# One row shift for each pair of heads in place of two, and the first product of a main score tile issued twice while no gated unit runs

## The chip, the cores and the metric

The kernel runs on one core of a Trainium2 chip. The time is device time in microseconds for one execution. Five engines work side by side, each through its own queue in order: TensorE (PE in the profile; its weight loads are PEld), VectorE (DVE), ScalarE (ACT), GpSimd (POOL) and SyncE (SP), which here only issues DMA transfers. Three runs of the kernel before gave 1223.69 to 1225.79 us, with a median of 1224.95.

## The reference

An attention with the queries averaged in twos, over 8 batches and 8 heads, followed by a gated unit with a spatial product. Cut to what matters:

```python
# q, k, v: (8, 8, 1152, 64)
q_pool = q.reshape(B, H, S // 2, 2, D).mean(axis=3)          # 576 queries
scores = scale * q_pool @ k.T                                # 576 x 1152
scores = scores - max(scores, axis=-1)                       # row shift
attn = exp(scores); attn = attn / (sum(attn) + 1e-9)
x = (attn @ v), heads side by side                           # (8, 576, 512)

h = relu(x @ w_in)                                           # 1024 wide
u, v = h[..., :512], h[..., 512:]
v_n = (v - mean(v)) / sqrt(var(v) + 1e-6)
v_s = einsum('ts,bsd->btd', w_spatial, v_n) + b_spatial
out = (u * v_s) @ w_out
```

## The kernel before

**Pairs.** The 64 heads are worked in 32 pairs: two heads of one batch lie on the 128 partitions (64 each). For pair `i` the kernel prepares the operands (`prep`), finds each query's largest score (`maxima`), computes scores and exponentials (`attention`), and multiplies by the values (`values`, `tail_values`). Numbers are held as a high and a low half, so most products are made of several.

**Maxima and shift.** The 2 x 576 = 1152 queries of a pair are 9 blocks of 128: blocks 0 to 3 are the first 512 of head 0, block 4 the last 64 of head 0 and the first 64 of head 1, blocks 5 to 8 the rest of head 1. `maxima` computes for each block three products of 384 keys (L617, in block 4 L608) into a PSUM bank and takes the row maximum of each with VectorE (L623), into `mt`. `shift(st, mt, a, z)` then takes blocks `a` to `z`: the maximum over three pieces (L635, `mx`), a transposition on TensorE (L639), subtraction and scaling (L642), a cast and a remainder (L645, L646, `mr`), and two DMA transfers on SP (L649) that put the two halves as two extra rows into `X` (the buffers `xq`). The score products read these rows, so that the shift is part of the product. `maxima` calls `shift` for blocks 0 to 4 when block 4 is done and for blocks 5 to 8 at its end.

**Attention.** A pair has 18 main tiles (9 chunks of 128 keys for each head, 512 queries) and 4 tail tiles for the remaining 64 queries. A main tile is two products into one PSUM bank `pss` of three: L796 on the high halves, which opens the sum, and L797 on the low halves and the shift rows. L797 is thus the first that waits for the shift of its queries. ScalarE then takes the exponential (L802, into one of eight buffers `pt`), GpSimd splits the result into two halves (L822), and 12 products with the values follow (L714, L720, L725).

**Gated units.** When 8 pairs are done (two batches), a gated unit over these batches is put into the list `units` (`gated_unit`) and runs in small steps beside the attention of later pairs; the last one runs alone at the end. During the first 8 pairs, and into the ninth, the list is empty. In that time the weights of the gated units are also turned from doubles into two halves (`load_weights`, `from_double`, `head`, `rest`), mostly on VectorE and ScalarE.

**What sets the order.** The program is written as generators that take turns: `maxima(i + 1)`, `values_ahead(i)` and `prep(i + 2)` advance with each step of `attention(i)`. At the end `Order.pin` goes through the whole program with a cost for each instruction, takes on each engine the earliest ready one (the first in the program among these), and fixes the order that results on all five engines. So an instruction added or removed in one place can move others everywhere. On the chip each engine works through its own fixed row and waits at an instruction until its inputs and its buffer are there.

Of the kernel before, what the change touches and what calls it, by code (L numbers as in the profile page):

```python
# [261 lines left out]
def attn_sgu_kernel(ctx: ExitStack, tc: tile.TileContext, qT, kT, v, w_in, w_spT, b_sp, w_out, out):  # L262
    nc = tc.nc
# [13 lines left out]
    NT = S2 // P  # L277
# [316 lines left out]
    def maxima(i):  # L594
        st = state[i]
        qhl, khh, X = st["qhl"], st["khh"], st["X"]
        W = KEYS // 3
        NB = W // P
        mt = sm.tile([P, NT, 3], F32, name="mt", bufs=2)
        for t in range(NT):  # L600
            for n in range(3):

                if units or (t + n) % 2:
                    pm = ps_m.tile([P, 512], F32, name="pm")
                else:
                    pm = ps_w.tile([P, 512], F32, name="pw")
                if t == 4:
                    nc.tensor.matmul(  # L608
                        pm[:, :W],
                        lhsT=qd[i % 2].rearrange("p h s -> p (h s)"),  # L610
                        rhs=st["kn"][:, n * NB : (n + 1) * NB, :],
                        start=True, stop=True,
                    )
                else:
                    h = 0 if t < 4 else 1
                    c0 = t * P if t < 4 else TAIL + (t - 5) * P
                    nc.tensor.matmul(  # L617
                        pm[:, :W],
                        lhsT=qhl[:, h, c0 : c0 + P],
                        rhs=khh[:, h, n * NB : (n + 1) * NB, :],  # L620
                        start=True, stop=True,
                    )
                nc.vector.reduce_max(out=mt[:, t, n : n + 1], in_=pm[:, :W], axis=AX.X)  # L623
                yield

            if t == 4:
                yield from shift(st, mt, 0, 5)
        yield
        yield from shift(st, mt, 5, NT)

    def shift(st, mt, a, z):
        X = st["X"]
        n = z - a
        mx = sm.tile([P, NT], F32, name="mx", bufs=2)
        nc.vector.reduce_max(out=mx[:, :n], in_=mt[:, a:z], axis=AX.X)  # L635
        yield
        yield
        pt = ps_m.tile([P, 512], F32, name="pm")
        nc.tensor.transpose(out=pt[:n, :P], in_=mx[:, :n], identity=ident)  # L639
        mr = sm.tile([NT, 2, P], F16, name="mr", bufs=2)  # L640
        m = pt[:n, :P]
        nc.vector.tensor_scalar(  # L642
            out=m, in0=m, scalar1=st["lnp"][:n], scalar2=1.0 / MROW, op0=ALU.subtract, op1=ALU.mult
        )
        nc.vector.tensor_copy(out=mr[:n, 0], in_=m)  # L645
        nc.vector.tensor_sub(mr[:n, 1], m, mr[:n, 0])  # L646
        for r in range(2):
            rows = X[D + r : D + r + 1].rearrange("p h s -> p (h s)")
            nc.sync.dma_start(out=rows[:, a * P : z * P], in_=mr[:n, r])  # L649
        yield  # L650


    MAINS = (slice(0, MAIN), slice(TAIL, S))
# [13 lines left out]
    units = []  # L667
# [91 lines left out]
    def tail_values(i):  # L759

        b, hp = divmod(i, NHP)
        ptl, vp = state[i]["ptl"], vps[i % 2]
        ps = ps_m.tile([P, 512], F32, name="pm")
        o = ps[:, : 2 * D1].rearrange("p (h d) -> p h d", d=D1)
        for c in range(NC):
            top = ptl.bitcast(BF16)[:, c].rearrange("p h s -> p (h s)")[:, 1::2]
            rst = ptl.bitcast(F16)[:, c].rearrange("p h s -> p (h s)")[:, 0::2]
            nc.tensor.matmul(o, lhsT=top, rhs=vp[:, :, c, D : D + D1], start=c == 0, stop=False)
            nc.tensor.matmul(o[:, :, 0:D], lhsT=top, rhs=vp[:, :, c, 0:D], start=False, stop=False)
            nc.tensor.matmul(o, lhsT=rst, rhs=vp[:, :, c, D : D + D1], start=False, stop=c == NC - 1)  # L770
        r = inverse(o[:, 0, D : D + 1], "dent")
        for h in range(2):
            rows = slice(h * D, (h + 1) * D)
            nc.vector.tensor_scalar_mul(xt[rows, hp, rows], o[rows, h, 0:D], r[rows])

    def turn(last=False):

        while todo and (last or len(todo) > LAG):
            if not last and todo[0][1] % NC == 0 and len(todo) <= LAG + 1:
                break  # L780
            values(*todo.popleft())
        for x in list(later):
            x[0] -= 1
            if x[0] <= 0 or last:
                later.remove(x)
                x[1]()

    def attention(i):

        st = state[i]  # L790
        qhl, khh, X, KL, esc = (st[n] for n in ("qhl", "khh", "X", "KL", "esc"))
        ptl = pt_.tile([P, NC, 2, TAIL], F32, name="ptl")
        st.update(ptl=ptl, pt=[])

        def products(o, c, h, q):
            nc.tensor.matmul(o, lhsT=khh[:, h, c, :], rhs=qhl[:, h, q], start=True, stop=False)  # L796
            nc.tensor.matmul(o, lhsT=KL[0:KR, h, c, :], rhs=X[0:KR, h, q], start=False, stop=True)  # L797

        def main_tile(pt, c, h):
            ps = ps_s.tile([P, MAIN], F32, name="pss")  # L800
            products(ps, c, h, MAINS[h])
            nc.scalar.activation(pt, ps, AF.Exp, bias=0.0, scale=esc)  # L802

        def tail_tile(h, n):
            ps = ps_s.tile([P, MAIN], F32, name="pss")
            a, z = CUT[n], CUT[n + 1]
            cols = [ps[:, (c - a) * TAIL : (c - a + 1) * TAIL] for c in range(a, z)]
            for c, x in zip(range(a, z), cols):
                nc.tensor.matmul(
                    x, lhsT=khh[:, h, c, :], rhs=qhl[:, h, TAILS[h]], start=c == a, stop=False, skip_group_check=True  # L810
                )
            for c, x in zip(range(a, z), cols):
                nc.tensor.matmul(  # L813
                    x, lhsT=KL[0:KR, h, c, :], rhs=X[0:KR, h, TAILS[h]], start=False, stop=c == z - 1,
                    skip_group_check=True,
                )
            o = ps[:, : (z - a) * TAIL].rearrange("p (c s) -> p c s", s=TAIL)
            nc.scalar.activation(ptl[:, a:z, h], o, AF.Exp, bias=0.0, scale=esc)  # L818

        def split(t):  # L820

            nc.gpsimd.tensor_sub(t.bitcast(F16)[..., 0::2], t, t.bitcast(BF16)[..., 1::2])  # L822

        for k in range(STEPS):
            h, c = divmod(k, NC)
            st["pt"].append(pp.tile([P, MAIN], F32, name="pt"))
            main_tile(st["pt"][k], c, h)
            split(st["pt"][k])
            yield
            todo.append((i, k))  # L830
            turn()
            yield
            if k in (1, 2, 3, 4):
                tail_tile((k - 1) % 2, (k - 1) // 2)
                yield
            if k == TAIL_SPLIT:
                split(ptl.rearrange("p c h s -> p c (h s)"))
            if k == TAIL_AT:
                tail_values(i)
# [258 lines left out]
    next(norms[3])  # L1098
    load_kq(1)
    first = maxima(0)  # L1100
    for _ in range(15):
        next(first)
# [9 lines left out]
    for i in range(NP):  # L1112
        if i + 2 < NP:
            load_kq(i + 2)
        run = [
            Pace(maxima(i + 1), MAX_RATE) if i + 1 < NP else None,
            Pace(values_ahead(i), V_RATE),
            Pace(prep(i + 2), PREP_RATE, PREP_AT) if i + 2 < NP else None,
            Pace(weights, W_RATE, W_AT if i == 0 else 0),
        ]  # L1120
        for _ in attention(i):
            for r in run:
                if r:
                    r.tick()
            credit = min(credit + MOE_RATE, 2.0)
            while credit >= 1 and units:
                credit -= 1
                unit_step()
        for r in run[:3]:
            if r:  # L1130
                drain(r.gen)
        weights = run[3].gen
        if ends_unit(i) and i < 2 * NHP:
            drain(weights)
            weights = None
            spatial_weights[0] = step(load_spatial())
# [50 lines left out]
```

## Time and profile before

| | |
|---|---|
| median of three runs | 1224.95 us |
| profiled execution | 1227.06 us |
| its span, first to last instruction | 1225.3 us |
| mean granted TensorE clock | 0.983 |
| first main product (L796) of pair 0 | 17.6 us |
| first main product of pair 8 | 275.4 us |
| last main product | 1119.2 us |

A profile line names the line of the kernel, the engine, the operation and the tiles, out<-in. A row of a timeline starts with its start and its length in us. A matmul's length includes the time from its start to its last result; matmuls overlap, so the rate of TensorE is read from the distance between starts. In a window's row each engine has its busy time; PEclk is the share of the TensorE clock that was granted.

### The profile page before, as it was taken

What the parts mean: (1) busy time and instruction counts of PE and PEld (TensorE: products, weight loads), DVE (VectorE), ACT (ScalarE), POOL (GpSimd) and SP (SyncE); (2) the same over time, 40 slices, a digit from 0 to 9 for tenths busy, and PEclk for the clock granted to TensorE, in tenths of its full rate; (3) what the DMA queues carried; (4) which work ended last, traced back from release to release, by engine and by line L of the source; (5) the groups of instructions that cost most, each with busy time, mean ns of one, the idle gap of its engine ahead of it and who ended that gap; (6) DMA issues with size and microseconds to landing.
All of it is one profiled execution on the core that took longest, in us unless ns stands there. A gap on an engine that the chain in (4) does not pass through costs nothing.

```text
span 1225.3 us, 34090 instructions
## 1 busy us (share of the span) xinstructions
PE 1153.0 (94%) x13632; PEld 725.7 (59%) x13632; DVE 906.2 (74%) x2187; ACT 889.2 (73%) x1659; POOL 875.8 (71%) x750
## 2 busy tenths in 40 slices
PE   3878888889999999999999999999999999999998
PEld 1545566556666666666666666566666666665453
DVE  5699999977889678766679686865669867851644
ACT  4788669778977877868777787878777876754433
POOL 2769979898887877777788877778887776764000
PEclk9899999999999999999999999999999999999999
DMA  5454454446333443155322442146422321111002
GB/s 188 157 180 133 118 180 123 110 115 173 113 89 94 133 126 101 51 145 170 93 75 75 132 134 74 53 133 198 113 75 75 90 84 43 30 45 36 1 1 78
DMA packets 62335, 126.70 MB, mean 103 GB/s; under 512 B 13728, under 2 KB 21920, under 8 KB 61664
## 3 DMA queue, kind: packets, MB, share of 16 engines
q1 hardware_dynamic: 62176, 124.52, 34.7%
q8 instruction: 107, 1.75, 0.6%
q14 instruction: 52, 0.43, 0.1%
HBM read 81.20 MB, written 9.44 MB: 74 GB/s over the span
## 4 chain that ended last, share of the span: by engine, by line
PE 72%; DVE 8%; ACT 2%; POOL 1%; issue 1%; DMA 1%; SPq 1%; ACTq 0%; DVEq 0%; POOLq 0%
PE pss L797 7%; PE pss L796 7%; PE pm L617 7%; PE pw L984 6%; PE pw L879 6%; PE pw L1027 6%; PE pw L943 5%; PE o L725 4%; PE o L714 4%; PE o L720 4%; DVE mt L623 3%; DVE vv L372 2%; PE pss L879 1%; PE pss L984 1%; PE pss L1027 1%
## 5 line engine op out<-in xcount | busy, mean ns | idle before, releaser
L822 POOL TENSOR_TENSOR pt<-pt 128x512 f16<-128x512 f32 x576 | 641.6, 1134 | 185.3 <-ACT pt L802 183.3
L802 ACT ACTIVATE pt<-pss,esc 128x512 f32<-128x512 f32 x576 | 387.7, 687 | 150.0 <-PE pss L797 114.3
L623 DVE TENSOR_REDUCE mt<-pm 128x1 f32<-128x384 f32 x733 | 387.1, 548 | 70.7 <-PE pm L617 61.9
L796 PE MATMUL pss<-qhi,khi 128*128 128x512 f16 x576 | 220.5, 384 | 13.9 <-ACT pt L802 12.8
L797 PE MATMUL pss<-xq,klo 66*128 66x512 f16 x576 | 221.1, 385 | 1.3 <-DMA xq<-mr 1.3
L617 PE MATMUL pm<-khi,qhi 128*128 128x384 f16 x655 | 205.5, 330 | 10.9 <-DVE mt L623 5.9
L714 PEld LDWEIGHTS <-pt 128*128 128x128 bf16 x2304 | 132.2, 99 | 69.1 <-issue 4.7
L725 PE MATMUL o<-vp,pt 128*128 128x65 f16 x2304 | 169.6, 194 | 2.5 <-POOL pt L822 2.4
L714 PE MATMUL o<-vp,pt 128*128 128x65 f16 x2304 | 170.8, 194 | 0.2
L720 PE MATMUL o<-vp,pt 128*128 128x64 f16 x2304 | 168.3, 194 | 0.0
L725 PEld LDWEIGHTS <-pt 128*128 128x128 f16 x2304 | 121.1, 99 | 26.9 <-POOL pt L822 5.0
L617 PEld LDWEIGHTS <-qhi 128*128 128x128 f16 x768 | 73.8, 99 | 81.9 <-issue 38.0
L720 PEld LDWEIGHTS <-pt 128*128 128x128 bf16 x2304 | 112.3, 99 | 3.3 <-issue 0.5
L879 PE MATMUL pw<-wi_h,xg 128*128 128x512 f16 x240 | 88.7, 378 | 0.2 <-DVE mt L623 0.2
L818 ACT ACTIVATE ptl<-pss,esc 128x256 f32<-128x256 f32 (+1 forms) x128 | 63.9, 499 | 27.8 <-PE pss L813 27.0
L822 POOL TENSOR_TENSOR ptl<-ptl 128x1152 f16<-128x1152 f32 x32 | 70.3, 2197 | 18.8 <-ACT ptl L818 18.8
L1027 PE MATMUL pw<-wo_h,vv 128*128 128x512 f16 x216 | 79.7, 379 | 3.9 <-DVE vv L372 3.9
L797 PEld LDWEIGHTS <-klo 66*128 66x128 f16 x576 | 57.1, 99 | 43.3 <-issue 17.4
L984 PE MATMUL pw<-ws_h,vv 128*128 128x512 f16 x216 | 80.6, 379 | 0.0
L943 PE MATMUL pw<-xg,wi_h 128*128 128x512 f16 (+1 forms) x336 | 80.6, 325 | 0.0
L623 DVE TENSOR_REDUCE mt<-pw 128x1 f32<-128x384 f32 x131 | 69.2, 541 | 11.1 <-PE pw L617 10.7
L796 PEld LDWEIGHTS <-khi 128*128 128x128 f16 x576 | 56.7, 99 | 21.0 <-issue 3.6
(194 smaller groups left out, 2446.1 us busy)
## 6 DMA issues: line engine op xcount, KB each, us to landing
vt<-in_v_dram SPq DMA_DIRECT2D x56, 576.0 KB
qt<-in_qT_dram SPq DMA_DIRECT2D x32, 576.0 KB
kt<-in_kT_dram SPq DMA_DIRECT2D x32, 576.0 KB
khi<-kn SPq DMA_DIRECT2D x128, 144.0 KB
out_dram<-row SPq DMA_DIRECT2D x24, 256.0 KB
qhi<-xq SPq DMA_DIRECT2D x64, 72.0 KB
klo<-klo SPq DMA_DIRECT2D x32, 144.0 KB
vv<-in_w_in_dram SPq DMA_DIRECT2D x4, 1024.0 KB
```

What stands on the lines that cost most here:

```text
L617: nc.tensor.matmul(pm[:, :W], lhsT=qhl[:, h, c0 : c0 + P], rhs=khh[:, h, n * NB : (n + 1) * NB, :], start=True, stop=True,)
L623: nc.vector.reduce_max(out=mt[:, t, n : n + 1], in_=pm[:, :W], axis=AX.X)
L714: nc.tensor.matmul(o[:, t], lhsT=top[:, cols], rhs=vp[:, D : D + D1], start=c == 0 and t == 0, stop=False, skip_group_check=True,)
L720: nc.tensor.matmul(o[:, t, 0:D], lhsT=top[:, cols], rhs=vp[:, 0:D], start=False, stop=False, skip_group_check=True)
L725: nc.tensor.matmul(o[:, t], lhsT=rst[:, cols], rhs=vp[:, D : D + D1], start=False, stop=c == NC - 1, skip_group_check=True,)
L796: nc.tensor.matmul(o, lhsT=khh[:, h, c, :], rhs=qhl[:, h, q], start=True, stop=False)
L797: nc.tensor.matmul(o, lhsT=KL[0:KR, h, c, :], rhs=X[0:KR, h, q], start=False, stop=True)
L802: nc.scalar.activation(pt, ps, AF.Exp, bias=0.0, scale=esc)
L822: nc.gpsimd.tensor_sub(t.bitcast(F16)[..., 0::2], t, t.bitcast(BF16)[..., 1::2])
L879: nc.tensor.matmul(ph, lhsT=xa[:, cc, c0 : c0 + P], rhs=wa[:, cc, DH:DF], start=n == 0, stop=n == 3 * NCC - 1,)
L984: nc.tensor.matmul(pv, lhsT=l, rhs=r[:, 0:MAIN], **fl)
L1027: nc.tensor.matmul(py, lhsT=ga[:, fc, c0 : c0 + P], rhs=wa[:, fc, :], start=m == 0, stop=m == end - 1)
```

## The change

`maxima` calls `shift` twice for the first pair only. For the others there is one call at the end, over all nine blocks. And `main_tile` issues the product of the high halves once more ahead of the two products, with `start` and `stop` set, as long as `units` is empty; the next product of the tile opens its sum anew and overwrites it.

```diff
                 nc.vector.reduce_max(out=mt[:, t, n : n + 1], in_=pm[:, :W], axis=AX.X)
                 yield

-            if t == 4:
+            if t == 4 and i == 0:
                 yield from shift(st, mt, 0, 5)
         yield
-        yield from shift(st, mt, 5, NT)
+        yield from shift(st, mt, 5 if i == 0 else 0, NT)
...
         def main_tile(pt, c, h):
             ps = ps_s.tile([P, MAIN], F32, name="pss")
+            if not units:
+                nc.tensor.matmul(ps, lhsT=khh[:, h, c, :], rhs=qhl[:, h, MAINS[h]], start=True, stop=True)
             products(ps, c, h, MAINS[h])
             nc.scalar.activation(pt, ps, AF.Exp, bias=0.0, scale=esc)
```

TensorE has 26714 rows before and 26981 after: 149 products with their weight loads more, 31 transpositions fewer. From line 802 on, the changed kernel's line numbers are two higher; the added product is its L802.

On VectorE the rows around the shift of pair 8, the first pair that is computed beside a gated unit, read as follows before (the shift of blocks 0 to 4, 498 rows ahead of it):

```order
L355 TENSOR_SCALAR qkr<-pm 128x2
L356 TENSOR_SCALAR qks<-pm 128x2
L635 TENSOR_REDUCE mx<-mt 128x5
L361 TENSOR_REDUCE wot<-woq 128x1
L623 TENSOR_REDUCE mt<-pw 128x1
L642 TENSOR_SCALAR pm<-pm,lnp 5x128
L350 TENSOR_SCALAR pm<-pm 128x1
L623 TENSOR_REDUCE mt<-pw 128x1
L556 TENSOR_SCALAR lnp<-lnp 128x1
L645 CAST mr<-pm 5x128
L372 SCALAR_TENSOR_TENSOR qhi_117<-qt,qks,xq_111 128x576
L646 TENSOR_TENSOR mr<-pm,mr 5x128
```

And after (the only shift of pair 8, 493 rows ahead of it):

```order
L623 TENSOR_REDUCE mt<-pw 128x1
L350 TENSOR_SCALAR pm<-pm 128x1
L635 TENSOR_REDUCE mx<-mt 128x9
L355 TENSOR_SCALAR wor<-pm 128x1
L356 TENSOR_SCALAR wos<-pm 128x1
L642 TENSOR_SCALAR pm<-pm,lnp 9x128
L645 CAST mr<-pm 9x128
L646 TENSOR_TENSOR mr<-pm,mr 9x128
L372 SCALAR_TENSOR_TENSOR wo_l<-u,wos,wo_h 128x1024
L623 TENSOR_REDUCE mt<-pw 128x1
L372 SCALAR_TENSOR_TENSOR wo_l<-u,wos,wo_h 128x1024
L623 TENSOR_REDUCE mt<-pm 128x1
```

The shift covers all nine blocks, the preparation of a later pair's queries (`qhi`) stands ahead of it now, and two remainders of the weights (`wo_l`) behind it.

On TensorE the first main tiles of pair 0 read before (`khi`, `qhi`: high halves; `pm`, `pw`: banks of the maxima):

```order
L617 MATMUL pm<-khi_114,qhi_117 128x384
L796 LDWEIGHTS khi_114
L796 MATMUL pss<-qhi_117,khi_114 128x512
L796 LDWEIGHTS khi_114
L796 MATMUL pss<-qhi_117,khi_114 128x512
L617 LDWEIGHTS qhi_117
L617 MATMUL pw<-khi_114,qhi_117 128x384
```

And after:

```order
L617 MATMUL pm<-khi_114,qhi_117 128x384
L802 LDWEIGHTS khi_114
L802 MATMUL pss<-qhi_117,khi_114 128x512
L796 LDWEIGHTS khi_114
L796 MATMUL pss<-qhi_117,khi_114 128x512
L617 LDWEIGHTS qhi_117
L617 MATMUL pw<-khi_114,qhi_117 128x384
L802 LDWEIGHTS khi_114
L802 MATMUL pss<-qhi_117,khi_114 128x512
L617 LDWEIGHTS qhi_117
L617 MATMUL pm<-khi_114,qhi_117 128x384
L796 LDWEIGHTS khi_114
```

The added product (L802) stands ahead of the tile's own first product, with other products between them in some tiles. Between a pair's transposition (L639) and its first L797, TensorE has 134 to 196 rows in pairs 9 to 31 after; before, in the same pairs, the second shift's transposition stands between 303 rows behind that L797 and 120 ahead of it.

## The prediction

> **What bounds the kernel now.** I read the page's head, then busy time by stretch, then single rows at the places that the change touches.
>
> ```profile
> span 1225.3 us, 34090 instructions
> PE 1153.0 (94%) x13632; PEld 725.7 (59%) x13632; DVE 906.2 (74%) x2187; ACT 889.2 (73%) x1659; POOL 875.8 (71%) x750
> ...
> PEclk9899999999999999999999999999999999999999
> ```
>
> TensorE is busy for most of the span, and its granted clock is below full only in the first quarter. So the kernel has at least two stages, and the windows (busy us of each engine, then the granted clock, DMA share and GB/s) tell them apart:
>
> ```profile
> core 0: us, PE busy (x) PEld busy (x) DVE busy (x) ACT busy (x) POOL busy (x), PEclk, DMA share, GB/s
> ...
> 30.00:61.00 31.00, 26.57 (x319) 17.14 (x317) 19.97 (x47) 22.75 (x43) 22.14 (x20) 0.80 0.47 152
> ...
> 92.00:153.00 61.00, 52.12 (x704) 34.52 (x703) 56.15 (x120) 46.12 (x84) 57.02 (x43) 0.95 0.42 125
> 153.00:214.00 61.00, 53.27 (x741) 36.68 (x739) 57.55 (x128) 50.36 (x95) 51.96 (x41) 0.96 0.51 153
> 214.00:275.00 61.00, 50.41 (x695) 33.83 (x696) 52.77 (x124) 46.85 (x84) 52.74 (x41) 0.94 0.41 112
> 275.00:1118.00 843.00, 832.69 (x10248) 533.71 (x10246) 620.73 (x1543) 646.14 (x1210) 661.48 (x575) 1.00 0.35 100
> 1118.00:1225.00 107.00, 103.39 (x661) 51.44 (x659) 51.48 (x121) 38.66 (x74) 2.94 (x3) 1.00 0.08 27
> ```
>
> From 92 to 275 us (pairs 3 to 7, no gated unit yet) VectorE is busy 56.15 + 57.55 + 52.77 = 166.5 of 183 us, 91%, and TensorE 155.8, 85%: VectorE leads there. From 275 on gated units run, TensorE is busy 832.69 of 843 us at full clock, and VectorE has 222 us to spare. So before 275 us a saving must be VectorE's, and after it TensorE's. The end is the start of pair 8 plus the TensorE work that is left then.
>
> Where the shifts stand against their pairs decides what joining them may cost. For pairs 3 and 8, the maxima over the row blocks (L635) of the first and second shift, the first second-product (L797) of the pair, and SP's transfers:
>
> ```profile
> 117.30 0.15 DVE L635 TENSOR_REDUCE mx<-mt 128x5 f32<-128x15 f32 x1
> 133.54 0.15 DVE L635 TENSOR_REDUCE mx<-mt 128x4 f32<-128x12 f32 x1
> ...
> 123.21 0.38 PE L797 MATMUL pss<-xq,klo 66*128 66x512 f16 x1
> ...
> 267.14 0.15 DVE L635 TENSOR_REDUCE mx<-mt 128x5 f32<-128x15 f32 x1
> 279.97 0.16 DVE L635 TENSOR_REDUCE mx<-mt 128x4 f32<-128x12 f32 x1
> ...
> 272.96 0.73 SPq L649 DMA_DIRECT2D xq<-mr  x1
> 281.47 1.34 SPq L649 DMA_DIRECT2D xq<-mr  x2
> ...
> 275.62 0.38 PE L797 MATMUL pss<-xq,klo 66*128 66x512 f16 x1
> ```
>
> Pair 3 starts at 123.21, ten us before VectorE comes to its second shift (133.54), and pair 8 at 275.62, four before (279.97). Today a pair starts on half of its maxima. After the change it can't.
>
> **The change, part by part.** *One shift.* Pairs 1 to 31 lose one shift each: on VectorE L635, L642, L645 and L646, on TensorE one transposition, on SP two transfers. The free size of the joined instructions stays 128, so I cost them as one of today's. VectorE's instructions overlap, so I take the distance between starts:
>
> ```profile
> 266.07 0.54 DVE L623 TENSOR_REDUCE mt<-pw 128x1 f32<-128x384 f32 x1
> 266.54 0.54 DVE L623 TENSOR_REDUCE mt<-pm 128x1 f32<-128x384 f32 x1
> ...
> 267.14 0.15 DVE L635 TENSOR_REDUCE mx<-mt 128x5 f32<-128x15 f32 x1
> 267.21 0.14 DVE L361 TENSOR_REDUCE wot<-woq 128x1 f32<-128x2 f32 x1
> ...
> 267.74 0.34 DVE L642 TENSOR_SCALAR pm<-pm,lnp 5x128 f32<-5x128 f32 x1
> 268.00 0.14 DVE L350 TENSOR_SCALAR pm<-pm 128x1 int32<-128x1 int32 x1
> ...
> 269.02 0.82 DVE L372 SCALAR_TENSOR_TENSOR qhi<-qt,qks,xq 128x576 f16<-128x576 f32 x1 [0.16 <-issue]
> 269.75 0.27 DVE L646 TENSOR_TENSOR mr<-pm,mr 5x128 f16<-5x128 f32 x1
> 269.95 0.14 DVE L355 TENSOR_SCALAR vr<-pm 128x1 int32<-128x1 int32 x1
> ```
>
> A shift is 0.07 (267.14 to 267.21) + 0.26 (267.74 to 268.00) + 0.20 (269.75 to 269.95) and the cast of the same size, 0.20: 0.73 us. A row-block maximum is 0.47 (266.07 to 266.54). All 31 shifts free 22.6 us of VectorE, but only those before pair 8 count, since later VectorE is not the bound.
>
> *When pair 8 can start.* In the program order VectorE has 498 rows ahead of pair 8's first shift before, and 493 ahead of its only shift after. The difference: 10 more row-block maxima (4.7 us); 7 shifts fewer (7 x 0.73 = 5.1); one more L372 on qhi (0.73, 269.02 to 269.75); 12 more small rows, at 0.07 each at the least (269.95 is such a row), at most 0.3: I take 1.5. Sum: 4.7 - 5.1 + 0.7 + 1.5 = +1.8 us, at 91% busy +2.0, so the shift stands at 267.1 + 2.0 = 269.1. Idle time goes too:
>
> ```profile
> DVE pm L642 <- PE pm L639: 6.0, 4, 3.1
> ```
>
> VectorE idled 6.0 us for the transposition in 51 to 275 us. With 7 or 8 shifts in place of 15 I take off 2.8: 266.3. From the maximum to the end of the last issue a second shift took 282.8 - 280.0 = 2.8 us; the first, with SP busy with the pair's other transfers, 273.7 - 267.1 = 6.6. The landing shows once, where TensorE waited for it:
>
> ```profile
> 212.50 0.73 SPq L649 DMA_DIRECT2D xq<-mr  x1
> ...
> 214.31 0.38 PE L797 MATMUL pss<-xq,klo 66*128 66x512 f16 x1 [1.31 <-DMA xq<-mr]
> ```
>
> That is 1.1 us after the issue ended (213.2). The path is thus 3.9 to 7.7 us; I take 5.5, nearer the second shift's, since the joined shift comes as late on SP. Pair 8 would start at 266.3 + 5.5 = 271.8, 3.8 us earlier than 275.62.
>
> *The product issued twice.* 149 main tiles get it: the 144 of pairs 0 to 7 and 5 of pair 8. What it costs is the distance between two such products:
>
> ```profile
> 493.18 0.38 PE L797 MATMUL pss<-xq,klo 66*128 66x512 f16 x1
> 493.40 0.38 PE L796 MATMUL pss<-qhi,khi 128*128 128x512 f16 x1
> ...
> 493.74 0.28 PE L714 MATMUL o<-vp,pt 128*128 128x65 f16 x4
> 493.86 0.28 PE L720 MATMUL o<-vp,pt 128*128 128x64 f16 x4
> 493.98 0.38 PE L797 MATMUL pss<-xq,klo 66*128 66x512 f16 x1
> ```
>
> 0.22 us each, 18 x 0.22 = 4.0 a pair, 32.8 in all. TensorE idles 183 - 155.8 = 27 us in 92 to 275, about 4.6 per pair at 31 us a pair, so the doubled products fit, barely, beside VectorE's work. If that cover were gone they would cost 32.8; if they also raised the clock, they could give time back (below). Nearest to the idle row is "hidden", but idle time is not always where a tile is issued, and each pair's start now waits at the head of TensorE's queue with the next pair's maxima (L617), the pair's other products and the values behind it, for which VectorE and ScalarE wait. For both I charge 3 us in this stage. Pair 8 then starts 0.8 us earlier.
>
> *What TensorE has left at pair 8.* By the order, counting from pair 8's first L797, 24 transpositions fewer are left, 68 value products (L714, L720, L725) fewer, since they stand earlier now, 2 row-block products fewer, and 4 doubled products more. A transposition's rate is seen in four in a row:
>
> ```profile
> 171.88 0.45 PE pm L747 x4
> ...
> L639 PE MATMUL pm<-ident,mx x47: 269/272/276, 280.5 to 1088.7; 128*4 128x128 f32 x24, 128*5 128x128 f32 x23
> ```
>
> 0.11 us each, 47 of them after 275: 24 x 0.11 = 2.6 us. Values are 0.03 (493.74 to 493.86 for four): 2.0. Row-block products (384 columns, three quarters of 0.22) 0.3, doubled ones -0.9. Sum 4.0 us less. TensorE has no slack there, so it counts in full.
>
> *The wait at later pairs.* From pair 9 on the first shift was far ahead of its pair; the joined one is near. Between its transposition and the pair's first L797 the order has 4.1 to 7.3 us of TensorE work (counted at 0.22 us per 512 columns). Against it, for pair 14's second shift:
>
> ```profile
> 489.01 0.17 DVE L635 TENSOR_REDUCE mx<-mt 128x4 f32<-128x12 f32 x1
> ...
> 493.28 1.34 SPq L649 DMA_DIRECT2D xq<-mr  x2
> ```
>
> 5.6 us from the maximum to the end of the issue, plus 1.1. It will mostly fit; three pairs (14, 22, 30) have only 4.1 us. I charge 1 us, with bounds of 0 and 23 x 1.3 (the one wait seen) = 30.
>
> Sum: -0.8 - 4.0 + 1.0 = **-3.8 us**. The profiled execution took 1227.06 us with a span of 1225.3; the median of the three runs is 1224.95. The forecast is 1224.95 - 3.8 = 1221.1.
>
> **A rule weighed.** The clock is 0.80 in 30 to 61 us and 0.94 to 0.96 in 92 to 275, where TensorE is busy 85%, and 1.00 from 275 on, where it is busy 99% (windows above). The Trainium skill (TensorE: Matmul & The Clock Gate, "Why this matters for your kernels") says that a gap of more than about 3 us between bursts of matmuls puts TensorE back to half clock. By that rule, with which these rows agree, a product issued beside its twin fills no gap, and a wait at a pair's start makes a new one, so it speaks against this change; with one half-clock stretch more per pair the first stage would be longer, as in the first rival below.
>
> **The rivals.**
> *A late gate (slower), 0.25.* TensorE stands blocked at each pair's first L797 for the 5.5 us path, VectorE uses up what lies in the four PSUM banks of row-block products (4 x 0.47 = 1.9 us) and then starves. It decides once less than about 5 us of other work stands behind the joined maximum on both engines. At 2 us a pair over pairs 1 to 8 the price is 16 in place of my 3: 1221.1 + 13 = 1234. For it: pair 3 starts ten us before its second shift today. Against it: in the new order (shown with the change) rests of the weights (L372) and further row-block maxima stand right behind the joined shift on VectorE.
> *No difference, 0.23.* The later pairs wait 0.17 us each more (23 x 0.17 = 4), or the doubled products cost 4 us more than hidden: about 1225.
> *The clock comes up, 0.10.* In 92 to 275 the clock's loss is 61 x (0.05 + 0.04 + 0.06) = 9 us of TensorE's time. If the doubled products raised it and VectorE idled 6 us less of its 16.5, the time were about 1215. The skill's rule, above, speaks against it.
> *The change doesn't do what it says.* The order shows 33 transpositions for 64, and 149 products more, so this is out.
>
> **How the numbers follow.** My forecast has 0.42. A measurement can tell about 0.2%, 2.4 us, from no change: faster is below 1222.5, slower above 1227.4. Faster: 0.42 + 0.10 = 0.52; same 0.23; slower 0.25. The range takes in the clock's case and most of the late gate's: 1212 to 1236.
>
> **What would show it.** Pair 8's first L797 near 275 us; VectorE's busy share in 92 to 275 still 90% or more; waits of L797 for the transfer of xq a few us in all; TensorE's busy share after pair 8 as high as now. It is wrong if L797 waits for that transfer by more than 10 us in all, if VectorE's share falls under 85% before pair 8, or if pair 8 starts later than 280.

## The result and the profile after

The changed kernel is **slower**: 1231.21 us in the median of five runs (1230.97 to 1236.36), against 1224.95 (1223.22 to 1226.88). The ratio is 1.0058, with a 95% interval of 1.004 to 1.0076. The forecast was 1221.1. The profiled execution is the longest of the five: 1236.36 us, with a span of 1234.6.

The page's head of the changed kernel, the lines shown of before:

```profile
span 1234.6 us, 34060 instructions
...
PE 1173.1 (95%) x13750; PEld 735.1 (60%) x13750; DVE 884.4 (72%) x2063; ACT 890.8 (72%) x1659; POOL 877.7 (71%) x750
...
PEclk9879998999999999999999999999999999999999
```

Its windows up to 275 us (busy us of PE, PEld, DVE, ACT, POOL, then clock, DMA share, GB/s), and behind them the first of these rows in the kernel before:

```profile
61.00:92.00 31.00, 19.93 (x186) 12.35 (x187) 27.01 (x58) 19.15 (x40) 9.36 (x8) 0.72 0.58 191
92.00:153.00 61.00, 54.35 (x716) 34.88 (x715) 56.30 (x107) 46.87 (x81) 55.67 (x42) 1.00 0.42 117
153.00:214.00 61.00, 55.50 (x702) 37.17 (x701) 53.89 (x114) 45.56 (x87) 50.59 (x39) 0.92 0.53 158
214.00:275.00 61.00, 55.91 (x723) 35.91 (x722) 56.91 (x111) 46.27 (x84) 53.95 (x41) 0.97 0.37 105
```

```profile
61.00:92.00 31.00, 23.59 (x238) 14.10 (x239) 30.54 (x68) 25.61 (x47) 19.91 (x16) 0.91 0.57 182
```

VectorE is as busy as before from 92 to 275 us (56.30 + 53.89 + 56.91 = 167.1, 91%), and TensorE busier. The row 61 to 92, which holds the start of pair 1, stands out: GpSimd works 9.36 of 31 us (19.91 before), so the split of exponentials nearly stops. A window alone doesn't tell how far the program is at its end. The rows of single places do. For pairs 3 and 8 of the changed kernel, the joined shift's maximum, its transfers, and the pair's first second-product:

```profile
135.51 0.18 DVE L635 TENSOR_REDUCE mx<-mt 128x9 f32<-128x27 f32 x1
...
142.38 0.38 PE L797 MATMUL pss<-xq,klo 66*128 66x512 f16 x1
...
289.67 0.18 DVE L635 TENSOR_REDUCE mx<-mt 128x9 f32<-128x27 f32 x1
...
291.15 1.61 SPq L649 DMA_DIRECT2D xq<-mr  x2
...
294.62 0.38 PE L797 MATMUL pss<-xq,klo 66*128 66x512 f16 x1
```

Pair 3 starts at 142.4 in place of 123.2, pair 8 at 294.6 in place of 275.6: both 19 us late. So nothing is lost on balance between them, and all of it ahead of pair 3. The first L797 (us) of some pairs, in these two kernels and in two experiments below, shows where:

| pair | before | changed | joined shift alone | both shifts late |
|---|---|---|---|---|
| 0 | 32.4 | 32.9 | 32.5 | 32.5 |
| 1 | 68.5 | 80.6 | 78.0 | 75.3 |
| 2 | 94.7 | 111.9 | 107.4 | 109.6 |
| 3 | 123.2 | 142.4 | 138.6 | 138.5 |
| 8 | 275.6 | 294.6 | 290.8 | 291.2 |

Pair 1 alone starts 12.1 us late, pair 2 17.2, pair 3 19.2. From pair 3 to pair 8 it is 152.4 us before, 152.2 in the changed kernel and with the joined shift alone, and 152.7 with both shifts late.

The end is only 9.3 us late (1234.6 - 1225.3), so 9.7 us come back after pair 8. To see both, I cut each span at pair 8's first L797 (before, then after):

```profile
0.00:275.60 275.60, 217.47 (x2735) 140.96 (x2736) 234.26 (x526) 205.00 (x377) 211.95 (x175) 0.93 0.48 145
275.60:1225.30 949.70, 935.49 (x10898) 584.72 (x10896) 671.95 (x1663) 684.20 (x1283) 663.82 (x576) 1.00 0.32 91
```

```profile
0.00:294.60 294.60, 243.68 (x2945) 154.76 (x2946) 245.00 (x509) 209.13 (x380) 216.35 (x177) 0.92 0.47 140
294.60:1234.60 940.00, 929.42 (x10806) 580.38 (x10804) 639.37 (x1554) 681.71 (x1280) 661.33 (x574) 1.00 0.32 91
```

After pair 8, TensorE has 6.1 us less busy time and 3.6 less idle (14.2 before, 10.6 after). Before pair 8 it has 26.2 more busy, 7.2 less idle. The question is which part of the change costs the 19 us, and why the saving that the forecast counted on was not there.

### The profile page after: what moved, and what is told of

Read it like the earlier page. It is cut to its first block, busy times and chain, and to the rows that moved or that the text cites. A ratio compares the mean times of both kernels' runs of the same rounds, so it can differ in the third digit from the quotient of the medians.

```text
span 1234.6 us, 34060 instructions
## 1 busy us (share of the span) xinstructions
PE 1173.1 (95%) x13750; PEld 735.1 (60%) x13750; DVE 884.4 (72%) x2063; ACT 890.8 (72%) x1659; POOL 877.7 (71%) x750
## 4 chain that ended last, share of the span: by engine, by line
PE 75%; DVE 11%; DMA 2%; ACT 2%; issue 1%; POOL 1%; SPq 0%; ACTq 0%; DVEq 0%; POOLq 0%
PE pss L797 8%; PE pss L796 8%; PE pm L617 7%; PE pw L986 7%; PE pw L881 6%; PE pw L945 6%; PE pw L1029 5%; PE o L725 4%; PE o L714 4%; PE o L720 4%; DVE mt L623 4%; DVE vv L372 1%; PE pss L802 1%; PE pm L747 1%; PE pss L881 1%; DMA vt<-in_v_dram 1%
## 5 line engine op out<-in xcount | busy, mean ns | idle before, releaser
L617 PE MATMUL pm<-khi,qhi 128*128 128x384 f16 x655 | 209.3, 331 | 12.6 <-DVE mt L623 6.7
L797 PE MATMUL pss<-xq,klo 66*128 66x512 f16 x576 | 219.9, 385 | 1.2 <-DMA xq<-mr 1.2
L714 PE MATMUL o<-vp,pt 128*128 128x65 f16 x2304 | 167.2, 193 | 4.0 <-DVE xm L733 4.0
L725 PE MATMUL o<-vp,pt 128*128 128x65 f16 x2304 | 169.1, 193 | 0.3 <-POOL pt L824 0.2
L617 PEld LDWEIGHTS <-qhi 128*128 128x128 f16 x768 | 73.9, 99 | 68.6 <-issue 27.8
L623 DVE TENSOR_REDUCE mt<-pw 128x1 f32<-128x384 f32 x131 | 69.6, 543 | 16.4 <-PE pw L617 15.4
L797 PEld LDWEIGHTS <-klo 66*128 66x128 f16 x576 | 56.9, 99 | 38.0 <-issue 7.3
L824 POOL TENSOR_TENSOR ptl<-ptl 128x1152 f16<-128x1152 f32 x32 | 68.6, 2143 | 15.2 <-ACT ptl L820 15.2
```

Of the source, the lines that this page charges most:

```text
L617: nc.tensor.matmul(pm[:, :W], lhsT=qhl[:, h, c0 : c0 + P], rhs=khh[:, h, n * NB : (n + 1) * NB, :], start=True, stop=True,)
L714: nc.tensor.matmul(o[:, t], lhsT=top[:, cols], rhs=vp[:, D : D + D1], start=c == 0 and t == 0, stop=False, skip_group_check=True,)
L725: nc.tensor.matmul(o[:, t], lhsT=rst[:, cols], rhs=vp[:, D : D + D1], start=False, stop=c == NC - 1, skip_group_check=True,)
```

## The experiments

Theory **gate**: a pair can't start before all its maxima, and in the first eight pairs they come too late for that. Theory **twice**: the 149 extra products are not hidden. Each ratio below is to the kernel before on the same chip, with its 95% interval. Only the places of the change are edited.

**The two parts apart.**

```diff
# joined shift alone
-            if t == 4:
+            if t == 4 and i == 0:
...
-        yield from shift(st, mt, 5, NT)
+        yield from shift(st, mt, 5 if i == 0 else 0, NT)
# product twice alone
             ps = ps_s.tile([P, MAIN], F32, name="pss")
+            if not units:
+                nc.tensor.matmul(ps, lhsT=khh[:, h, c, :], rhs=qhl[:, h, MAINS[h]], start=True, stop=True)
```

> The joined shift alone, no product twice. Gate theory (a pair can't start before all its maxima, and this costs in the first eight pairs): the first stage is still long, pair 8's first L797 at 285 us or later, time 1225 to 1235. Twice theory (the 149 extra products load TensorE in the first stage, the gate is free): pair 8 starts near 272, time 1219 to 1223.

> The product issued twice, with two shifts for each pair as before. Gate theory: within 2.5 us of before (1222 to 1228), pair 8 near 275. Twice theory: slower, 1230 or more, pair 8 later than 282. Clock rival: fewer half-clock stretches before 275 us and a time under 1222.

The joined shift alone gave **1.0037** (1.0018 to 1.0057), pair 8 at 290.8 us; the product twice alone **1.0043** (1.0027 to 1.0058), pair 8 at 276.4. Each theory is right for a part, and neither part is free; but the twice theory had put pair 8 later than 282, and it isn't, and the gate theory had put the product within 2.5 us of before (it cost 5.3). Together they gave 1.0058; the sum would be 1.0080, and the intervals don't tell the two apart. The first stage of the joined shift alone, cut at pair 8:

```profile
0.00:290.80 290.80, 230.53 (x2809) 149.02 (x2810) 244.40 (x513) 210.22 (x385) 218.71 (x179) 0.89 0.47 142
290.80:1229.40 938.60, 926.73 (x10794) 578.48 (x10792) 639.58 (x1551) 679.19 (x1274) 656.97 (x572) 1.00 0.32 91
```

It starts pair 8 15.2 us late without one extra product, and gets 11.1 back: less work is left on TensorE (busy 926.73 for 935.49) and it idles less (11.9 for 14.2).

**Where the joined shift costs.** The shift is joined only from pair 9 on, the same with the product twice, or only in pairs 1 to 8.

```diff
-            if t == 4:
+            if t == 4 and (i < 9):                # third: i == 0 or i > 8
...
-        yield from shift(st, mt, 5, NT)
+        yield from shift(st, mt, 5 if i < 9 else 0, NT)
```

> The joined shift from pair 9 on, two shifts in pairs 0 to 8, no product twice. Gate theory: first stage as before (pair 8 near 275), and after it 23 transpositions of 0.11 us and part of the idle time saved: 1218 to 1223. If the late pairs' wait costs (my charge of 1 us too small): 1226 or more.

> The joined shift from pair 9 on, and the product twice. Gate theory: as the joined shift from pair 9 alone, within 3 us. Twice theory: slower than it by 6 us or more.

> The joined shift in pairs 1 to 8 alone, two shifts in the others, no product twice. If the gate costs in the first stage and nowhere else: the joined shift everywhere gave 1.0037 and from pair 9 on 0.997, so this gives about 1.0067, some 8 us, with pair 8's first L797 at 288 us or later. If the cost of the joined shift were spread over all pairs: under 1.003.

From pair 9 on: **0.997** (0.9955 to 0.9985), 1222.18 us in the median, the only version found that beats the kernel before. With the product twice: 1.001 (0.9997 to 1.0024), 5.7 us more in the median, nearly the 6 of the twice theory, so the product costs about 0.4% there too. Only pairs 1 to 8: **1.0095** (1.0066 to 1.0124), pair 8 at 287.8. The joined shift costs in pairs 1 to 8, and the later ones gain. The two sum to 1.0065, where the whole gave 1.0037; the interval of the third is 0.3% to either side, so the difference may be noise, or come from the order, which is another one in each version.

**The gate without the saving.** Both shifts stay, but in pairs 1 to 8 both come at the end of the maxima.

```diff
-            if t == 4:
+            if t == 4 and not 0 < i < 9:
                 yield from shift(st, mt, 0, 5)
         yield
-        yield from shift(st, mt, 5, NT)
+        if 0 < i < 9:
+            for _ in zip(shift(st, mt, 0, 5), shift(st, mt, 5, NT)):
+                yield
+        else:
+            yield from shift(st, mt, 5, NT)
```

> Two shifts for each pair, as before, but in pairs 1 to 8 both are made at the end of the pair's maxima: the gate of the joined shift without its saving of instructions. Gate theory: at least as slow as the joined shift in pairs 1 to 8 (1.0095), that is 1.008 or more, pair 8's first L797 at 285 us or later. If it is the form of the joined instructions (nine blocks in one) that costs: within 0.3% of before.

**1.012** (1.0095 to 1.0145), pair 8 at 291.2. So the late start costs, not the form of the joined instructions. What it doesn't separate is the wait itself from the order that `Order.pin` plans around it: every version with a late gate has an order of its own.

**The gate earlier.** The maxima run ahead at 1.5 per step, with the joined shift everywhere, and, in the first eight pairs, with the shift joined from pair 9 on.

```diff
-    MAX_RATE = 1.0
+    MAX_RATE = 1.5
# second kernel: in its place
-            Pace(maxima(i + 1), MAX_RATE) if i + 1 < NP else None,
+            Pace(maxima(i + 1), 1.5 if i < 8 else MAX_RATE) if i + 1 < NP else None,
```

> The joined shift alone (no product twice), and the maxima run ahead at 1.5 per step of the attention in place of 1.0, so that the shift is ready earlier against its pair. If the gate is what costs: pair 8's first L797 earlier than the 290.8 us of the joined shift alone by 8 us or more and a time under 1226. If VectorE's work alone sets the first stage: pair 8 at 285 or later still, and a time above 1228.

> The joined shift from pair 9 on, no product twice, and in the first eight pairs the maxima run ahead at 1.5 per step. If the early stage gains by earlier maxima with the loose gate too: under 0.995. If earlier maxima help only against the gate: about 0.997, as the joined shift from pair 9 on alone.

The first: 1.0011 (0.9993 to 1.003), 1225.99 us, just under the 1226 that was expected, and pair 8 at 272.7, 18 us earlier than with the joined shift alone. That is the gate again. But the stretch after pair 8 is 950.3 us in place of 938.6: two thirds of it are given back. The second: 1.001 (0.9995 to 1.0025), neither number that was expected. With the gate open, earlier maxima didn't help; they made it worse (0.997 without).

**The extra product: its time, or the new order?** The order is planned with a cost for each instruction, so both can be separated. First the extra product is one column wide, but planned as if it were full: the rows of the product twice, with hardly any of its work. Then it is full, but planned at nothing: without it, the rows of before. Then one column in this old order. The traces bear the orders out: without the extra products, VectorE, ScalarE and GpSimd have the same rows, and TensorE the same products, as before in the second and third, and as with the product twice in the first. Last, it is issued two times more, with its cost.

```diff
# one column, planned as 512 (in Order.cost)
             n = count(xs[0])
+            if n == 1 and xs[0].dtype == F16:
+                n = 512
...
+                nc.tensor.matmul(ps[:, :1], lhsT=khh[:, h, c, :], rhs=qhl[:, h, m0 : m0 + 1], start=True, stop=True)
# full, planned at nothing (in Order.pin; the extra products' names are in self.free)
-        cost = [self.cost(e, i) for e, i in zip(lane, prog)]
+        cost = [(0.0, 0.0) if i.name in self.free else self.cost(e, i) for e, i in zip(lane, prog)]
```

> Two shifts, the extra product one column wide, but put in order as if it were 512 wide: every engine has the rows of the kernel with the product twice, and TensorE is spared nearly all of the extra work. Theory A, the new order costs: slower than before by about as much as the product twice, 1.004. Theory B, the extra work costs: within 0.15% of before.

> Two shifts, the extra product at full width but put in order as if it took no time: without it every engine has the rows of before in the order of before. Theory A, the new order costs: within 0.15% of before, or faster if the higher clock helps. Theory B, the extra work costs: 1.004 or more.

> Two shifts, the extra product one column wide, in the order of before (as the full one in the old order, which gave 1.0087). Theory B, the time of the extra product costs: within 0.2% of before. If the number of instructions or the earlier take of the bank costs: 1.004 or more.

> Two shifts, the first product of a main tile issued three times while no gated unit runs. Theory B, the extra work costs: TensorE has 298 x 0.22 = 65 us more before pair 8 and idled about 67 us there, so the first stage turns TensorE-bound: more than twice the cost of the product twice (1.0043), 1.012 or more. If the higher clock paid for it: 1.006 or less.

| extra product | order | ratio | 95% |
|---|---|---|---|
| full | new | 1.0043 | 1.0027 to 1.0058 |
| one column | new | 1.0019 | 1.0005 to 1.0033 |
| full | of before | 1.0087 | 1.0068 to 1.0106 |
| one column | of before | 0.9989 | 0.997 to 1.0008 |
| full, twice more | its own | 1.0094 | 1.0074 to 1.0115 |

The time of the product costs: 0.98% in the order of before (1.0087 against 0.9989), as theory B has it. In the new order it costs 0.24% (1.0043 against 1.0019), and the order itself some 0.2%, more than the 0.15% that theory B allowed and half of what theory A asked for. So the new order hides most of the product's time, and with its own cost about half is left. The thrice issued product lies under the 1.012 expected and over the 1.006: about twice the cost of the product twice. (TensorE's idle time before pair 8, 67 us in that expectation, is 58.1 by the windows above.) What hid it and what didn't is read from the first stage of the full product in the old order, and in the new:

```profile
0.00:284.00 284.00, 239.39 (x2881) 152.42 (x2882) 235.95 (x526) 207.81 (x378) 211.42 (x175) 0.95 0.47 141
```

```profile
0.00:276.40 276.40, 232.97 (x2940) 149.58 (x2941) 241.07 (x534) 207.65 (x382) 214.53 (x177) 0.98 0.49 147
276.40:1228.00 951.60, 934.87 (x10842) 583.09 (x10840) 668.70 (x1654) 682.94 (x1278) 664.30 (x574) 1.00 0.31 90
```

In the old order TensorE's idle time falls from 58.1 us (275.6 - 217.47) to 44.6 only. Its busy time rises by 21.9 us, less than the 33 of the extra products; the clock, 0.95 for 0.93, is a part of the difference, and the rest stays open. Of the 21.9, 13.5 lie in time that was idle, and pair 8 starts 8.4 us late. In the new order idle falls to 43.4 and the clock rises from 0.93 to 0.98, and pair 8 starts 0.8 late. In this execution 1.9 us more are lost after pair 8 (951.60 for 949.70). That is 2.7 us; the timed runs say 5.3, and the rest isn't explained by this one trace.

## Why the prediction was wrong, step by step

**The stages and what bounds them** were read rightly from 92 us on. (Pair 2 starts at 94.7, so these windows hold pairs 2 to 7, not 3 to 7.) What stands ahead of them, the starts of pairs 1 and 2, was left out, and there the time was lost. That the end is "the start of pair 8 plus the TensorE work that is left then" held: after pair 8 TensorE was busy 98 to 99% in every traced run.

**"When pair 8 can start" is the step that failed.** It put the joined shift of pair 8 at 266.3 us: 1.8 us of VectorE work more, 2.8 of its idle time less. It stood at 289.7, and at 286.1 with the joined shift alone, which shows the step without the extra products. The prediction counted VectorE's rows ahead of pair 8 and reckoned them at the pace of 92 to 275 us. But pair 1 now waits for its second half of maxima. TensorE before that start, in the kernel before and in the changed one:

```profile
68.50 0.38 PE L797 MATMUL pss<-xq,klo 66*128 66x512 f16 x1
```

```profile
71.40 0.28 PE L639 MATMUL pm<-ident,mx 128*9 128x128 f32 x1 [1.82 <-DVE mx L635]
...
75.23 0.48 PE L617 MATMUL pm<-khi,qhi 128*128 128x384 f16 x1 [3.06 <-DVE mr L646]
77.56 0.48 PE L617 MATMUL pw<-khi,qhi 128*128 128x384 f16 x1 [1.85 <-DVE mt L623]
79.90 0.48 PE L617 MATMUL pm<-khi,qhi 128*128 128x384 f16 x1 [1.86 <-DVE mt L623]
...
80.64 0.63 PE L797 MATMUL pss<-xq,klo 66*128 66x512 f16 x1
```

The joined maximum comes at 71.16, where the first shift's came at 61.3, and TensorE idles 8.6 us around it: first for the maximum, then in front of the row-block products of pair 2 (L617), which stand ahead of pair 1's L797 in its row and wait for VectorE. Before, pair 1 started on its first shift alone. Pairs 2 and 3 add 5.1 and 2.0 us to the 12.1 of pair 1, and pair 8 is as late as pair 3. No run joins the shift in pairs 1 to 3 alone, so why the later pairs add nothing stays open.

The same lag, seen in VectorE's busy and idle time, is split by its windows up to the shift of pair 8 (before to its first shift, then the joined shift alone):

```profile
0.00:267.10 267.10, 210.96 (x2647) 136.30 (x2648) 228.70 (x506) 196.61 (x362) 205.83 (x169) 0.92 0.49 148
```

```profile
0.00:286.10 286.10, 225.91 (x2746) 146.00 (x2747) 240.08 (x503) 206.57 (x379) 214.01 (x176) 0.89 0.47 141
```

Busy time rose by 11.4 us, not 1.8, and idle time rose by 7.6 (38.4 to 46.0) where 2.8 less was forecast. Idle time first: I let the wait for the transposition go and took the rest as it was. But TensorE has its row in order, and where it stands in front of a pair's start, VectorE waits for it elsewhere. (It hardly stands at L797 itself: L797's waits for the transfer are 2.7 us in the whole changed kernel and 0.6 with the joined shift alone.) The joined shift alone, VectorE's longest waits from 30 to 286 us:

```profile
DVE mt L623 <- PE pw L617: 7.1, 7, 4.3
DVE dent L693 <- PE pm L770: 6.4, 6, 1.8
DVE pm L350 <- PE pm L345: 4.5, 2, 3.7
DVE den L693 <- PE o L725: 4.5, 3, 3.2
DVE mt L623 <- PE pm L617: 3.9, 6, 1.2
DVE pm L642 <- PE pm L639: 2.0, 1, 2.0
```

And before, from 30 to 267 us:

```profile
DVE pm L642 <- PE pm L639: 8.1, 5, 3.1
DVE mt L623 <- PE pw L617: 6.1, 4, 4.3
DVE dent L693 <- PE pm L770: 4.0, 3, 2.3
DVE pm L350 <- PE pm L345: 3.1, 1, 3.1
DVE mt L623 <- PE pm L617: 1.1, 3, 0.6
```

The wait for the transposition fell from 8.1 to 2.0, more than forecast, but the other waits of this list rose from 14.3 to 26.4. Busy time next. The groups of the remainders (L372) up to the same place, before and with the joined shift alone (busy us, mean ns):

```profile
L372 DVE SCALAR_TENSOR_TENSOR klo<-kt,qks,kn 128x640 f16<-128x640 f32 (+1 forms) x16 | 14.4, 911 | 0.0
L372 DVE SCALAR_TENSOR_TENSOR qhi<-qt,qks,xq 128x576 f16<-128x576 f32 x9 | 8.8, 978 | 1.9 <-ACT xq L369 1.1 <-POOL pt L822 0.6 <-issue 0.2
L372 DVE SCALAR_TENSOR_TENSOR vp<-vt,vs,vp 128x576 f16<-128x576 f32 x8 | 8.2, 1028 | 0.0
```

```profile
L372 DVE SCALAR_TENSOR_TENSOR klo<-kt,qks,kn 128x640 f16<-128x640 f32 (+1 forms) x16 | 19.2, 1208 | 0.0
L372 DVE SCALAR_TENSOR_TENSOR qhi<-qt,qks,xq 128x576 f16<-128x576 f32 x10 | 13.0, 1303 | 1.2 <-ACT xq L369 1.1
L372 DVE SCALAR_TENSOR_TENSOR vp<-vt,vs,vp 128x576 f16<-128x576 f32 x8 | 9.5, 1196 | 0.0
```

The same remainders, one more of them, take 41.7 us in place of 31.4: 10.3 more, of which I had 0.7. The trace shows what lengthens one. GpSimd's split and VectorE's remainder of the joined shift alone:

```profile
277.62 1.05 POOL L822 TENSOR_TENSOR pt<-pt 128x512 f16<-128x512 f32 x1
```

```profile
278.03 1.25 DVE L372 SCALAR_TENSOR_TENSOR qhi<-qt,qks,xq 128x576 f16<-128x576 f32 x1
279.21 0.54 DVE L623 TENSOR_REDUCE mt<-pm 128x1 f32<-128x384 f32 x1
```

The remainder ends at 279.28, 0.61 us after the split (278.67); before, an undisturbed one of this size took 0.82 in all (269.02, in the prediction). It waits for the split that runs. The traces up to that place bear it out: a remainder of queries, keys or values that starts while no GpSimd instruction runs takes 0.74 to 0.88 us in both kernels, and one that starts behind a running one up to 1.62 before and 1.72 with the joined shift. There are 18 of the latter in 41 before, and 25 in 42 with the joined shift. The Trainium skill (SBUF — State Buffer, "Who interferes with whom") says that a VectorE instruction with two SBUF inputs contends with a GpSimd instruction that reads SBUF; the trace agrees (0.82 us alone, 1.25 behind the split). So a busy VectorE was in part a waiting one, and 91% busy told less than I took from it. That the collisions grew because the gate lined the pairs' work up anew is argued from these rows; no run took them away.

**The product issued twice.** "Hidden", with 3 us charged for it and the gate together. Alone it cost 0.43%, 5.3 us, and in the order of before 0.87%, 10.7. The idle time on which I counted was real (58.1 us before pair 8), but in the order of before only 13.5 of it took in the extra products.

**What TensorE has left, and the later wait.** 4.0 us less and 1.0 for waits, so -3.0. The run that has only this part, the shift joined from pair 9 on, gave -0.30%, -3.7 us (interval -5.5 to -1.8): the size was right. Its one trace splits it otherwise: pair 8 starts at 278.4, 2.8 late, and 6.1 us are gained after it (943.6 for 949.7), 3.3 of them busy time of TensorE. In the changed kernel the stretch after pair 8 got 9.7 shorter, as more of the work stood ahead of pair 8 and idle time fell by 3.6. The one wait of a later pair's start is there and small:

```profile
PE pss L797 <- DMA xq<-mr: 1.2, 1, 1.2
```

**The path of a shift** was taken as 5.5 us and measured 5.0 for pair 8 (289.67 to 294.62), but 9.5 for pair 1 (71.16 to 80.64), which no term of the sum held.

**The rivals.** The late gate, 13 us above the forecast's time, named the right cause: in pairs 1 to 8 alone it cost 0.95%, 11.6 us, and 14.7 without the saving. That its price came near is luck in part: it was reckoned as 2 us for each of eight pairs with TensorE blocked at L797, and what showed is 9.5 us at pair 1, 15.4 by pair 3, and no more from there to pair 8 (joined shift alone), with TensorE waiting ahead of L797. I gave it 0.25 and should have given it the most: pair 3's second shift, ten us behind its pair's start, was quoted in the prediction and then treated as lag that the stage could lose for nothing. "The clock comes up" came true as far as the clock goes, with the product twice alone, and brought no net gain (last section). Of the three signs of being wrong only the start of pair 8 after 280 showed. The time lies inside the range of 1212 to 1236; the sign was wrong.

## What to carry to other kernels

Where two halves of a dependence are issued apart and the second half comes after the consumer has started, joining them closes a gate: price it by the distance between the consumer's start and the second half's end in the trace, before counting saved instructions. In the kernel before, the second shift's maximum of pairs 1, 2 and 3 comes 4.6, 9.8 and 10.3 us behind the pair's start; the joined shift alone made these pairs 9.5, 12.7 and 15.4 us late, that is 3 to 5 us more than the distance. Look at the first place where the gate closes, not only at the steady stretch: here the loss was made there. A saving and a gate can be put in different stages: the same edit gained 0.3% where the second half mostly came ahead of the consumer's start, and cost 1% where it came behind it. Idle time in an engine's row hides extra work only as far as that work stands near it: here 13.5 of 58.1 us were used.

## What the runs showed of the hardware

With the product twice the granted clock is full from 92 to 275 us, where it was 0.94 to 0.96. The product twice alone:

```profile
92.00:153.00 61.00, 56.37 (x753) 36.52 (x751) 58.60 (x126) 46.82 (x84) 55.77 (x42) 1.00 0.43 127
153.00:214.00 61.00, 58.16 (x775) 38.82 (x772) 59.50 (x133) 49.91 (x95) 54.05 (x42) 1.00 0.54 159
214.00:275.00 61.00, 54.70 (x769) 36.56 (x769) 54.72 (x123) 48.23 (x86) 53.76 (x42) 1.00 0.40 111
```

It is the work that does it, and not the order: in the order of before, the clock is 0.97 in all three windows with the full product, and 0.95, 0.94 and 0.90 with one column. So a product beside its twin does raise the clock; the way I applied the Trainium skill's rule on gaps in the prediction, that it fills none, was wrong. Short stretches of the kernel before show why:

```profile
52.43:55.84 3.41, 2.16 (x23) 0.93 (x23) 3.41 (x11) 0.00 (x0) 3.33 (x4) 1.00 0.88 330
55.84:59.25 3.41, 3.41 (x64) 3.24 (x61) 0.89 (x2) 2.66 (x6) 3.41 (x5) 0.50 1.04 407
...
117.30:120.70 3.40, 1.88 (x11) 0.78 (x9) 3.40 (x12) 3.40 (x8) 3.40 (x3) 1.00 0.01 3
120.70:124.10 3.40, 3.40 (x36) 2.41 (x36) 3.40 (x6) 2.25 (x3) 3.40 (x4) 1.00 0.26 58
124.10:127.50 3.40, 1.34 (x9) 0.48 (x8) 3.32 (x12) 0.00 (x0) 3.40 (x3) 1.00 0.89 203
127.50:130.90 3.40, 3.40 (x66) 3.40 (x65) 3.40 (x5) 2.00 (x3) 2.25 (x3) 0.50 0.57 185
```

After 3.4 us with TensorE busy for 1.34 the clock halves for the next 3.4; after 1.88 it stays. So the stretch need not be idle: in this kernel, from 60 us to pair 8, the six stretches of 3.4 us at full clock that were followed by half clock had TensorE busy for 0.98 to 1.73 us, and after those with 1.81 or more the clock stayed. It isn't the whole rule: an earlier one, from 52.43 us on, was busy for 2.16 and the clock halved all the same. What else decides is open.
